# A written-out order that reaches further, two batches' k and v in other buffers, and one chunk decoded once: slot attention with a Gelu feed-forward on one core

## The chip, the cores and the metric

The kernel runs on one core of a Trainium2 chip. The core has a matrix engine (TensorE, PE in the profile; its weight loads are PEld), a vector engine (VectorE, DVE), a scalar engine with function tables (ScalarE, ACT), a general engine (GpSimd, POOL) and SyncE (SP), which here issues all data transfers (DMA). Each engine takes its instructions in the order of its own queue and waits on semaphores for the others. The metric is the device time of the whole program in microseconds (us).

## What is computed

The input has 8 batches of 8 heads, 576 positions, 64 features a head; `phi` gives each position 32 weights over memory slots.

```python
a = softmax(phi, axis=2)                       # over the positions
k_m = einsum('bhsm,bhsd->bhmd', a, k)          # 32 slots per head
v_m = einsum('bhsm,bhsd->bhmd', a, v)
attn = softmax(scale * q @ k_m^T)              # over the 32 slots
x = (attn @ v_m), heads side by side           # 4608 x 512
out = gelu(x @ w_in) @ w_out                   # 512 -> 2048 -> 512
```

The softmaxes subtract their maxima and add 1e-9 to their sums. The two weight matrices come as float64. Each is read as pairs of 32-bit words and decoded on the core into float32 parts.

## The kernel before

**Work per batch.** `x @ w_in` is never formed by itself. For each batch the kernel first folds v_m into w_in: U = v_m · w_in, one small product per head pair, in four tiles of 512 hidden columns (`U`, 8 KB a partition each, split into a high and a low part). With the attention weights p (also split into high and low) a *hidden half* h.b.f.hf is six matmuls of 288 columns: for chunk f of 128 hidden units and half hf of the positions (`hidden`, line 696). ACT applies Gelu (lines 706 to 709), the result is split into gh and gl (lines 164 and 715), and a *product* p.b.f is twelve matmuls of 512 columns into four PSUM accumulators (`project`, line 728): gh with the high and low part of w_out, gl with the high part, for four blocks of 128 positions. The last 64 positions of each batch are kept in `tails` and multiplied for two batches at once behind every second batch.

**Order of the batches.** There are 16 chunks f. Batches 0 and 1 are done in two rounds, since the weights arrive and are decoded meanwhile: chunks 0 to 7 of batch 0, chunks 0 to 7 of batch 1, then chunks 8 to 15 of batch 0 and of batch 1. After the first round the accumulators are copied out as partial sums (`o.b.j.7`, tiles `part`), and added at the end of the second (`o.b.j.15`, line 766). From batch 2 on a batch runs through all 16 chunks.

**Pieces.** The program is written as small named pieces; the table near the end of the function gives what each does. Those that matter here: `Lphi`, `Lkv`, `Lq`, `Lwi`, `Lwo` load by DMA; `amax`, `aexp`, `anorm` and `Lphin`, `dg`, `pn`, `anat` are the softmax of phi, the latter four on a transposed copy `aT` (lines 353 to 380); `slots` is the product with k and v (line 397), `km` scales it, `slotsT` and `kT` turn it round; `score`, `sT`, `max`, `sub`, `exp`, `sum`, `inv`, `mul`, `pT`, `ph`, `pl` are the attention of one half (batch 0 has its own `n_` pieces); `Up`, `Uh`, `Ul` make a piece of U. `dB`, `dC`, `dG`, `dS` decode a weight chunk (ACT lines 204 and 205; DVE lines 209, 213 and 219), each for one of the two matrices (`dB.5.1`: w_out of chunk 5) or for both at once (`dB.15`); `dDi`, `dDo` add the parts on POOL, `dE` and `dF` split w_out into high (ACT or DVE) and low (line 245). `W.k.i` is one matmul on constant ones, whose result is not used. A letter behind a colon moves a piece's work to another engine (`d` DVE, `a` ACT).

**What sets the order.** `START` is a list of pieces, run in that order; their instructions are tied to it, engine by engine, by order edges. It covers everything up to h.0.13, p.0.12 and dF.15. What it does not name is put into a plan with due times and handed to the framework's scheduler, with edges that keep a piece from running more than two steps ahead. So up to about a fifth of the time the order is fixed, and behind that it is the scheduler's.

**Buffers.** Tag `U` has `NU = 5` slots of 8 KB a partition: U tiles, the raw words of a weight chunk under decoding, and batch 0's k and v lie there. Tag `kv` has `NK = 8` slots of 2 KB: one chunk of 128 positions of k and v, or one partial sum. Batches 0 and 1 leave four partial sums each there, until their second rounds end. Batch 2's k and v (five chunks for each of two groups of heads) are planned for that time. PSUM has one pair of banks for all of `slots`, `score`, `U`, `pn` and `slotsT`, two banks for hidden halves, and four accumulators. A DMA waits in SP's queue until its buffer is free, and all behind it wait too.

Of the kernel before, what the change touches and what calls it, by code (L numbers as in the profile page):

```python
# [24 lines left out]
atc.0.0.0 atc.0.0.4 W.4.16 dG.0.1 at.0.1.4 atc.0.1.4 dS.0.1 Lkv0.0.0 slots.0.0.0 W.3.1
anorm.0 km.0.0.0 Lkv0.1.0 slots.0.1.0 dDo.0 dE.0 W.3.8 W.3.9 dF.0 km.0.1.0 Lwi.0 dB.0.0
Lq.0.0 W.4.19 Lwo.1 slotsT.0.0 kT.0.0 dC.0.0 dB.1.1 Lq.0.1 dS.0.0 dG.0.0 W.3.19 dC.1.1
dS.1.1 dG.1.1 W.3.25 n_score.0 n_max.0 n_sub.0 n_score.1 dDi.0 n_exp.0 Lphi.1.0 Lwi.1
dB.1.0 Lwo.2 dB.2.1 amax.1.0 W.3.29 n_sum.0 dDo.1 aexp.1.0 n_inv.0 n_mul.0 n_max.1
n_score.2 n_sub.1 Lkv0.0.1 slots.0.0.1 dG.1.0 dC.1.0 dC.2.1 dS.2.1 dE.1 dF.1 n_exp.1  # L30
dG.2.1 km.0.0.1 dDo.2 Lkv0.1.1 n_sum.1 n_inv.1 slots.0.1.1 km.0.1.1 slotsT.0.1 kT.0.1
Lphi.1.1 W.3.34 amax.1.1 n_mul.1 dS.1.0 Lwi.2 dB.2.0 n_max.2 Up.0.0.1 Uh.0.0:d Ul.0.0
Lwi.3 n_T.0 n_sub.2 dE.2 dDi.1 n_T.1 Lwo.3 aexp.1.1 Up.0.1.1 W.2.2 n_hi.0 dC.2.0 dS.2.0
dG.2.0 n_exp.2 Uh.0.1:d Ul.0.1 dDi.2 n_lo.0 n_sum.2 n_inv.2 Lkv.1.0.0 W.2.12 at.1.0.0
Lkv.1.0.1 Lwo.4 dB.3.1 dC.3.1 dB.3.0 dG.3.1 at.1.1.0 atc.1.1.0 dF.2 atc.1.0.0 n_hi.1
h.0.0.0 dC.3.0 n_mul.2 dG.3.0 at.1.0.4 dS.3.0 Lkv.1.0.2 atc.1.0.4 dS.3.1 Lkv.1.0.3
Lkv.1.0.4 at.1.1.4 atc.1.1.4 n_lo.1 dDi.3 n_T.2 n_hi.2 dB.4.1 dC.4.1 Lkv.1.1.0 anorm.1
slots.1.0 n_lo.2 gelu.0.0.0 dDo.3 Lkv.1.1.1 km.1.0 h.0.0.1 dS.4.1 dG.4.1 Up.0.2.1
Uh.0.2:d Lwi.4 gelu.0.0.1 dE.3 gh.0.0:a h.0.1.0 Ul.0.2 gl.0.0 gelu.0.1.0 dB.4.0
Lkv.1.1.2 dF.3 Lkv.1.1.3 Lkv.1.1.4 h.0.1.1 gelu.0.1.1 Lwi.5 dC.4.0 slots.1.1 km.1.1  # L40
h.0.2.0 dG.4.0 Lwo.5 Lq.1.0 Lwi.6 dDo.4 dE.4 slotsT.1 dS.4.0 dF.4 kT.1 dB.5.0 h.0.2.1
Up.0.3.1 Uh.0.3:d Ul.0.3 gh.0.1:a gl.0.1 Lwi.7 Lwo.7 dB.5.1 dG.5.1 dDi.4 Lwi.8 dC.5.1
gelu.0.2.0 dS.5.1 dDo.5 p.0.0 score.1.0 sT.1.0.0 sT.1.0.1 max.1.0 gelu.0.2.1 gh.0.2:a
h.0.3.0 gelu.0.3.0 sub.1.0 Lwo.6 gl.0.2 h.0.3.1 Up.0.4.1 gelu.0.3.1 p.0.1 dG.5.0 dC.5.0
dS.5.0 Uh.0.4 Ul.0.4 exp.1.0 sum.1.0 inv.1.0 mul.1.0 h.0.4.0 gh.0.3:a dB.6.0 gl.0.3
dC.6.0 dE.5 dF.5 gelu.0.4.0 dDi.5 dB.6.1 h.0.4.1 Up.0.5.1 Uh.0.5:d Ul.0.5 p.0.2 Lq.1.1
score.1.1 dG.6.0 dS.6.0 dDi.6 pT.1.0 sT.1.1.0 sT.1.1.1 max.1.1 gelu.0.4.1 dB.7.0 h.0.5.0
gelu.0.5.0 ph.1.0 gh.0.4 dG.7.0 dC.6.1 h.0.5.1 Up.0.6.1 dS.6.1 Uh.0.6 Ul.0.6 sub.1.1
p.0.3 gl.0.4 dC.7.0 dS.7.0 gelu.0.5.1 dDi.7 gh.0.5:a gl.0.5 dG.6.1 h.0.6.0 Up.1.0.4
p.0.4 h.0.6.1 gelu.0.6.0 dB.7.1 Uh.1.0 Ul.1.0 dC.7.1 Up.0.7.1 exp.1.1 Uh.0.7 p.0.5  # L50
dS.7.1 dDo.6 dE.6:d dF.6 dG.7.1 gelu.0.6.1 gh.0.6:a dDo.7 dE.7 sum.1.1 Ul.0.7 inv.1.1
h.0.7.0 gelu.0.7.0 Lwo.8 dB.8.1 mul.1.1 pl.1.0 pT.1.1 gl.0.6 Up.1.4.4 dF.7 dC.8.1
h.0.7.1 gelu.0.7.1 gh.0.7:a dS.8.1 ph.1.1:d h.1.0.0 gl.0.7 Uh.1.4:d p.0.6 Lwo.9 pl.1.1
dB.8.0 dC.8.0 dS.8.0 dG.8.1 p.0.7 Lwi.9 o.0.0.7 h.1.0.1 gelu.1.0.0 dB.9.0 dB.9.1
gelu.1.0.1 h.1.1.0 dC.9.1 dS.9.1 o.0.1.7 h.1.1.1 gh.1.0 gl.1.0 dG.8.0 Ul.1.4 dC.9.0
o.0.3.7 dDo.8 dS.9.0 dE.8:d gelu.1.1.0 gelu.1.1.1 gh.1.1 o.0.2.7:a p.1.0 h.1.2.0
gelu.1.2.0 gl.1.1 dDi.8 dG.9.0 h.1.2.1 gelu.1.2.1 dF.8 Lwi.10 dB.10.0 dC.10.0 Lwi.11
gh.1.2 dS.10.0 gl.1.2 Lwo.10 dB.10.1 p.1.1 h.1.3.0 dC.10.1 dG.9.1 dDi.9 dDo.9 h.1.3.1
gelu.1.3.1 Lwi.12 gelu.1.3.0 gh.1.3:a gl.1.3 p.1.2 h.1.4.0 h.1.4.1 gelu.1.4.0 dE.9:d
gelu.1.4.1 h.1.5.0 dS.10.1 Lwo.11 p.1.3 Lwo.12 dG.10.0 dDi.10 dG.10.1 gelu.1.5.0  # L60
gh.1.4:a gl.1.4 dF.9 dB.11.0 h.1.5.1 p.1.4 dDo.10 dE.10:d h.1.6.0 dF.10 gelu.1.5.1
gh.1.5 gl.1.5 Lwi.13 p.1.5 dC.11.0 dB.11.1 dS.11.0 dG.11.0 dB.12.1 dC.12.1 dG.12.1
dB.12.0 dC.11.1 dDi.11 dS.11.1 gelu.1.6.0 h.1.6.1 gelu.1.6.1 dG.11.1 Lwo.13 Up.0.8.4
gh.1.6:a gl.1.6 h.1.7.0 dDo.11 dE.11 h.1.7.1 dS.12.1 gelu.1.7.0 dF.11 dB.13.0 gelu.1.7.1
dDo.12 dE.12 Uh.0.8:d p.1.6 dC.13.0 Lwo.14 Ul.0.8 h.0.8.0 dG.12.0 Lwi.14 h.0.8.1
gelu.0.8.0 dC.12.0 h.0.9.0 dB.13.1 gh.1.7 gl.1.7 gelu.0.9.0 dG.13.0 Up.1.8.4 dS.12.0
gelu.0.8.1 gh.0.8:a gl.0.8 dDi.12 dC.13.1 dS.13.1 p.1.7 o.1.0.7:a dG.13.1 dS.13.0 dDi.13
o.1.1.7 Uh.1.8 Ul.1.8 h.0.9.1 Lwo.15 h.0.10.0 gelu.0.9.1 gh.0.9:a gl.0.9 o.1.2.7:a
gelu.0.10.0 dF.12 h.0.10.1 gelu.0.10.1 o.1.3.7 p.0.8 dB.14.1 gh.0.10 dC.14.1 Up.0.12.2
dDo.13 dB.14.0 dE.13:d dS.14.1 p.0.9 Lwi.15 h.0.11.0 dF.13 Uh.0.12 dG.14.1 gl.0.10  # L70
# [9 lines left out]
def slot_attention_gelu_ffn(  # L80
# [180 lines left out]

    def load_kv(b, g, c):
        rows = rows_of(b, c)
        t = sb.tile([P, 2, 4, D], F32, tag="kv", name=f"kv_{b}_{g}_{c}", bufs=NK)
# [1 line left out]
        nc.sync.dma_start(t[:rows], kv[b, g, r : r + rows])
# [698 lines left out]
```

## Time and profile before

| | |
|---|---|
| median of 3 runs | 732.03 us (731.23 to 732.37) |
| the profiled execution: its own time | 731.3 us |
| its span (first to last instruction) | 729.5 us |
| granted clock of PE, mean | 0.986 |
| PE busy | 710.9 us (97%), 4998 matmuls |
| DVE busy | 391.4 us (54%) |
| ACT busy | 333.3 us (46%) |
| POOL busy | 47.1 us (6%) |
| moved by DMA | 65.15 MB |

A line of the profile names a source line, an engine, an operation, the tile written and the tile read, sizes and a count. In a timeline the first two numbers are start and duration in us, and a bracket at the end gives how long the engine had been idle and who released it. In a table of windows each row begins with the stretch and its length; then come busy times of the engines, PE's granted clock, the share of the DMA engines and GB/s. Matmuls overlap in the records, so the durations of single matmuls add up to more than the time they take, and a busy PE is not always a PE at its pace: a product of twelve matmuls takes 2.77 us when nothing holds it.

### The profile page before, as it was taken

How to read it: one execution, taken by the hardware profiler on the slowest of the kernel's cores; microseconds unless marked ns; L12 is line 12 of the kernel's file. 1: busy time of each engine (PE TensorE's matmuls, PEld its weight loads, DVE VectorE, ACT ScalarE, POOL GpSimd, SP SyncE). 2: the span in 40 equal slices, each digit the busy share in tenths (PEclk: the TensorE clock that was granted, in tenths of full speed). 3: DMA queues.
4: the chain of work that ended last, by engine and by line, in shares of the span. 5: the costliest groups of instructions: out<-in, count | busy, mean ns of one | idle time of the engine just before them, and what ended most of it. 6: DMA issues, size and time to landing. Idle time of an engine off the chain costs nothing.

```text
span 729.5 us, 12271 instructions
## 1 busy us (share of the span) xinstructions
PE 710.9 (97%) x4998; PEld 582.9 (80%) x4998; DVE 391.4 (54%) x701; ACT 333.3 (46%) x694; POOL 47.1 (6%) x45
## 2 busy tenths in 40 slices
...
GB/s 317 294 334 30 88 202 142 73 0 203 124 106 90 178 100 59 65 175 62 33 1 81 173 63 33 1 206 62 1 1 59 48 33 1 1 58 0 1 1 72
DMA packets 28760, 65.15 MB, mean 89 GB/s; under 512 B 2848, under 2 KB 6560, under 8 KB 28704
## 3 DMA queue, kind: packets, MB, share of 16 engines
...
q14 instruction: 17, 0.14, 0.1%
...
## 4 chain that ended last, share of the span: by engine, by line
PE 91%; DMA 4%; DVE 2%; ACT 1%; issue 1%; SPq 0%; ACTq 0%; DVEq 0%
PE acc L728 48%; PE h L696 28%; PE tacc L728 6%; PE pu L457 5%; DMA kv<-kv 2%; DMA raw<-w_out 1%; PE psc L397 1%; PE psc L457 1%; PE pk L397 1%; DVE o L766 0%; PE pt L337 0%; DVE raw L213 0%; PE tn L369 0%; DVE aT L376 0%; PE tn L423 0%
## 5 line engine op out<-in xcount | busy, mean ns | idle before, releaser
L696 PE MATMUL h<-p_hi,U 128*128 128x288 f32 x1024 | 205.5, 299 | 4.0 <-ACT tails L709 4.0
L728 PE MATMUL acc<-wo_hi,gh 128*128 128x512 f32 x512 | 204.1, 399 | 0.0
L728 PE MATMUL acc<-wo_lo,gh 128*128 128x512 f32 x512 | 201.4, 393 | 0.0
L728 PE MATMUL acc<-wo_hi,gl 128*128 128x512 f32 x512 | 201.2, 394 | 0.1
L696 PEld LDWEIGHTS h<-p_hi,U 128*128 128x128 f32 x1024 | 164.6, 189 | 22.3 <-ACT tails L709 6.1
L706 ACT ACTIVATE gf<-h 128x288 f32<-128x288 f32 x128 | 52.7, 412 | 240.0 <-issue 169.5
L164 DVE CAST gh<-gf 128x512 fp32r<-128x512 f32 x115 | 48.8, 425 | 195.8 <-ACT gf L708 194.4
L728 PEld LDWEIGHTS acc<-wo_hi,gh 128*128 128x128 f32 x512 | 96.4, 188 | 36.8 <-DVE gh L164 7.5
L728 PEld LDWEIGHTS acc<-wo_hi,gl 128*128 128x128 f32 x512 | 96.0, 188 | 23.1 <-DVE gl L715 1.0
L696 PE MATMUL h<-p_lo,U 128*128 128x288 f32 x512 | 109.7, 296 | 1.3 <-DVE p_lo L552 1.3
L728 PEld LDWEIGHTS acc<-wo_lo,gh 128*128 128x128 f32 x512 | 96.4, 188 | 17.4 <-issue 0.4
L715 DVE TENSOR_TENSOR gl<-gf,gh 128x512 fp32r<-128x512 f32 x128 | 89.5, 699 | 13.9 <-ACT gh L164 5.8
L696 PEld LDWEIGHTS h<-p_lo,U 128*128 128x128 f32 x512 | 83.4, 189 | 2.2 <-DVE p_lo L552 1.5
L708 ACT ACTIVATE gf<-h 128x224 f32<-128x224 f32 x128 | 45.7, 357 | 48.3 <-PE h L696 48.2
L659 DVE TENSOR_TENSOR U<-pu,U 128x1024 fp32r<-128x1024 f32 (+2 forms) x39 | 40.1, 1029 | 15.1 <-ACT U L164 15.0
L706 ACT ACT_TABLE_LOAD x27 | 34.6, 1283 | 11.1 <-issue 6.3
L457 PE MATMUL pu<-w_in_sb,kT 64*32 64x512 f32 (+2 forms) x624 | 37.0, 531 | 0.4 <-POOL w_in_sb L239 0.4
L164 ACT CAST U<-pu 128x1024 fp32r<-128x1024 f32 (+2 forms) x31 | 29.3, 944 | 16.2 <-PE pu L457 16.2
L709 ACT ACTIVATE tails<-h 128x64 f32<-128x64 f32 x128 | 28.5, 222 | 0.0
L565 DVE STREAM_TRANSPOSE sT<-psc 128x288 f32<-128x288 f32 x28 | 11.9, 462 | 30.4 <-PE psc L397 24.5
L204 ACT ACTIVATE y<-raw 128x512 f32<-128x512 f32 (+1 forms) x33 | 22.8, 690 | 8.8 <-DMA raw<-w_out 3.2
L239 POOL TENSOR_TENSOR w_in_sb<-y,raw 128x512 int32<-128x512 int32 x16 | 22.7, 1418 | 57.2 <-DVE y L219 35.9
...
## 6 DMA issues: line engine op xcount, KB each, us to landing
kv<-kv SPq DMA_DIRECT2D x68, 256.0 KB, 5.1
...
```

The source lines that it names most:

```text
L164: return e.copy(dst, src) if e is nc.scalar else e.tensor_copy(dst, src)
L204: nc.scalar.activation(y, high.bitcast(F32), AF.Abs, scale=2.0**16)
L239: nc.gpsimd.tensor_tensor(w, y, low, op=ALU.add)
L397: nc.tensor.matmul(pk[32 * j : 32 * j + 32, w0 * D : (w0 + n) * D], st["aT", b][:rows, c, g, 32 * j : 32 * j + 32], t[:rows, w0 : w0 + n, ...
L457: nc.tensor.matmul(ps[g][M * j : M * j + M], st["kT", b][rows, t, M * j : M * j + M], moving[rows, j, :], start=True, stop=True,)
L659: nc.vector.tensor_sub(u[:, :, 1], st["pu", b, f], u[:, :, 0].bitcast(F32))
L696: i = nc.tensor.matmul(h[:, :HS], u[g][w], x[:, g, :], start=(n == 0), stop=(n == 3 * G - 1))
L706: nc.scalar.activation(gf[:, :HS], h[:, :HS], AF.Gelu)
L708: nc.scalar.activation(gf[:, HS:], h[:, : MAIN - HS], AF.Gelu)
L709: nc.scalar.activation(tails()[:, f, b % 2], h[:, MAIN - HS : HS], AF.Gelu)
L715: nc.vector.tensor_tensor(g_of("gl", b, f), g_of("gf", b, f), g_of("gh", b, f).bitcast(F32), op=ALU.subtract)
L728: nc.tensor.matmul(acc, x, w[:, f, :], start=(first and n == 0), stop=(last and n == 2))
```

## The change

Three things are changed.

1. `START` is replaced by a longer list in another order. It now reaches p.1.15, the last product of batch 1's second round. The additional pieces are those that the plan held: the last chunks of batches 0 and 1, batch 2's preparation (phi, k, v, slots, scores, p, and the first U tile) and the first loads of batch 3. In the part that both lists cover, pieces change places, 17 of the 20 `W` pieces are gone, and some 45 pieces change between ACT and DVE.
2. `load_kv` puts chunks 0 to 3 of batch 2's k and v, for each of the two groups, into one tile of tag `U`. Chunk 4 stays in a `kv` slot.
3. `dB.15`, `dC.15`, `dS.15` and `dG.15`, which decode both matrices of chunk 15 although `dB.15.0` to `dG.15.1` have done so, are no longer in the list.

The beginning of the new list (up to h.0.0.0), its part from p.0.10 on and the edit of `load_kv`:

```diff
-Lphi.0.1 W.4.2 W.4.3 W.4.5 Lphi.0.0 W.4.7 W.4.9 W.4.11 W.4.12 Lwo.0 amax.0.1 aexp.0.1
-W.4.13 amax.0.0 aexp.0.0 W.4.14 dB.0.1 dC.0.1 at.0.0.0 at.0.1.0 atc.0.1.0:d at.0.0.4
...
-gh.0.12:a dG.15.1 dS.14.0 dB.15 dG.14.0 gl.0.12 p.0.11 dC.15 dS.15 dDi.14 Up.0.14.2
-Uh.0.14:d p.0.12 dDo.14 dE.14:d dG.15 h.0.13.0 Ul.0.14 h.0.13.1 gelu.0.13.0 gelu.0.13.1
-gh.0.13 gl.0.13 dF.14 dDo.15 dE.15:d dF.15
+W.4.3 Lphi.0.0 amax.0.0 aexp.0.0 at.0.0.0 Lphi.0.1 amax.0.1 aexp.0.1 anorm.0 atc.0.0.0:d
+at.0.1.0 atc.0.1.0 at.0.0.4 Lwo.0 at.0.1.4 atc.0.1.4:d Lkv0.0.0 Lkv0.1.0 atc.0.0.4:d
+slots.0.0.0 Lwo.1 Lq.0.0 Lq.0.1 dB.0.1 dC.0.1 dG.0.1 dS.0.1 dDo.0 dE.0:d dF.0
+slots.0.1.0 km.0.0.0 km.0.1.0 Lwi.1 dB.1.1 W.4.13 dC.1.1 dS.1.1 dG.1.1 dDo.1 dE.1:d dF.1
+slotsT.0.0 kT.0.0 n_score.0 n_max.0 n_sub.0 dB.1.0 dC.1.0 dS.1.0 n_score.1 dG.1.0 Lwi.0
+n_exp.0 n_sum.0 W.3.29 dB.0.0 n_inv.0 dC.0.0 dS.0.0 Lkv0.0.1 dG.0.0 slots.0.0.1 km.0.0.1
+n_max.1 n_sub.1 n_exp.1 n_mul.0 Lkv0.1.1 slots.0.1.1 Lphi.1.0 amax.1.0 n_sum.1 Lwi.2
+km.0.1.1 Lphi.1.1 n_inv.1 n_mul.1 dDi.0 Lwo.2 slotsT.0.1 kT.0.1 aexp.1.0 Up.0.0.1
+Lkv.1.0.0 dDi.1 dB.2.0 Uh.0.0:d Ul.0.0 dC.2.0 amax.1.1 aexp.1.1 dG.2.0 dS.2.0 Lkv.1.0.1
+n_score.2 Up.0.1.1 Uh.0.1:d Lkv.1.0.2 Lwo.3 n_T.0 n_T.1 Ul.0.1 dDi.2 Lkv.1.0.3 n_max.2
+n_sub.2 dB.2.1 dG.2.1 dC.2.1 at.1.1.0 dS.2.1 n_hi.0 at.1.0.0 Lkv.1.0.4 n_lo.0 h.0.0.0
...
+gh.0.11 dC.15.1 p.0.10 dC.14.0 dS.14.0 dDi.14 aexp.2.0 Lkv.2.0.3 Lkv.2.0.2 Ul.0.12
+Lkv.2.0.0 h.0.12.0 gl.0.11 h.0.12.1 gelu.0.12.1 gelu.0.12.0 gh.0.12:a dC.15.0 aexp.2.1
+dG.15.0 p.0.11 h.0.13.0 dS.15.0 gl.0.12 dS.14.1 dDi.15 Up.0.14.2 h.0.13.1 dS.15.1 dg.2
+Lkv.2.0.1 Uh.0.14:d Ul.0.14 dDo.14 gelu.0.13.1 gelu.0.13.0 gh.0.13 gl.0.13 p.0.12
+h.0.14.0 dG.15.1 dDo.15 h.0.14.1 gelu.0.14.0 h.0.15.0 Lq.2.0 p.0.13 dE.14 gelu.0.14.1
+h.0.15.1 pn.2 Lkv.2.0.4 dF.14 gelu.0.15.0 h.1.8.0 gelu.0.15.1 gh.0.14 gl.0.14 gh.0.15:a
+dE.15 anat.2 p.0.14 h.1.8.1 gelu.1.8.1 gl.0.15 Lkv.2.1.0 dF.15 p.0.15 o.0.0.15
+gelu.1.8.0 gh.1.8 o.0.1.15 o.0.2.15 h.1.9.0 h.1.9.1 gelu.1.9.1 slots.2.0 anorm.2 km.2.0
+gelu.1.9.0 gl.1.8 h.1.10.0 gelu.1.10.0 Lkv.2.1.1 Lkv.2.1.4 gh.1.9:a gl.1.9 Lkv.2.1.2
+Lkv.3.0.0 Up.1.12.4 o.0.3.15 p.1.8 p.1.9 Uh.1.12 Lkv.2.1.3 Ul.1.12 slots.2.1 h.1.10.1
+gelu.1.10.1 km.2.1 slotsT.2 h.1.11.0 kT.2:d score.2.0 gelu.1.11.0 h.1.11.1 gelu.1.11.1
...
+inv.2.1 gelu.1.14.0 mul.2.1 gelu.1.14.1 gh.1.14 pT.2.1 gl.1.14 ph.2.1 h.1.15.0 amax.3.0
+h.1.15.1 gelu.1.15.0 pl.2.1 p.1.14 gelu.1.15.1 gh.1.15 amax.3.1 gl.1.15 tg.1.0 p.1.15
```

```diff
     def load_kv(b, g, c):
         rows = rows_of(b, c)
-        t = sb.tile([P, 2, 4, D], F32, tag="kv", name=f"kv_{b}_{g}_{c}", bufs=NK)
+        if b == 2 and c < NT:
+            t = tile_of(
+                ("kvU", g),
+                lambda: sb.tile([P, NT, 2, 4, D], F32, tag="U", name=f"kvU_2_{g}", bufs=NU),
+            )[:, c]
+        else:
+            t = sb.tile([P, 2, 4, D], F32, tag="kv", name=f"kv_{b}_{g}_{c}", bufs=NK)
```

More of the change, by code (lines that the diff above doesn't have):

```diff
@@ L22 @@
 START = """
-Lphi.0.1 W.4.2 W.4.3 W.4.5 Lphi.0.0 W.4.7 W.4.9 W.4.11 W.4.12 Lwo.0 amax.0.1 aexp.0.1
-W.4.13 amax.0.0 aexp.0.0 W.4.14 dB.0.1 dC.0.1 at.0.0.0 at.0.1.0 atc.0.1.0:d at.0.0.4
[L25 to L70, printed above, removed]
@@ L71 @@
-dB.15.0 dC.15.0 gelu.0.11.0 Ul.0.12 dG.15.0 h.0.11.1 gelu.0.11.1 dS.15.0 dDi.15 dB.15.1
-dC.15.1 dS.15.1 gh.0.11 gl.0.11 h.0.12.0 gelu.0.12.0 dC.14.0 h.0.12.1 gelu.0.12.1 p.0.10
-gh.0.12:a dG.15.1 dS.14.0 dB.15 dG.14.0 gl.0.12 p.0.11 dC.15 dS.15 dDi.14 Up.0.14.2
-Uh.0.14:d p.0.12 dDo.14 dE.14:d dG.15 h.0.13.0 Ul.0.14 h.0.13.1 gelu.0.13.0 gelu.0.13.1
-gh.0.13 gl.0.13 dF.14 dDo.15 dE.15:d dF.15
+W.4.3 Lphi.0.0 amax.0.0 aexp.0.0 at.0.0.0 Lphi.0.1 amax.0.1 aexp.0.1 anorm.0 atc.0.0.0:d
+at.0.1.0 atc.0.1.0 at.0.0.4 Lwo.0 at.0.1.4 atc.0.1.4:d Lkv0.0.0 Lkv0.1.0 atc.0.0.4:d
@@ new lines @@
+Lkv.1.0.0 dDi.1 dB.2.0 Uh.0.0:d Ul.0.0 dC.2.0 amax.1.1 aexp.1.1 dG.2.0 dS.2.0 Lkv.1.0.1
+n_score.2 Up.0.1.1 Uh.0.1:d Lkv.1.0.2 Lwo.3 n_T.0 n_T.1 Ul.0.1 dDi.2 Lkv.1.0.3 n_max.2
+n_sub.2 dB.2.1 dG.2.1 dC.2.1 at.1.1.0 dS.2.1 n_hi.0 at.1.0.0 Lkv.1.0.4 n_lo.0 h.0.0.0
+atc.1.1.0 Lkv.1.1.0 atc.1.0.0:d at.1.0.4 n_exp.2 n_sum.2 n_inv.2 n_mul.2 atc.1.0.4:d
+dB.3.1 n_hi.1 dC.3.1 dDo.2 dG.3.1 dS.3.1 dDo.3 anorm.1 at.1.1.4 n_T.2 atc.1.1.4
+gelu.0.0.0 n_hi.2 Lwi.3 slots.1.0 km.1.0 Lkv.1.1.1 n_lo.2 n_lo.1 h.0.0.1 dB.3.0 dC.3.0
@@ new lines @@
+dS.3.0 dE.2 Up.0.2.1 Lkv.1.1.2 gelu.0.0.1 Lwo.4 Uh.0.2 Lkv.1.1.3 h.0.1.0 gelu.0.1.0
+h.0.1.1 dG.3.0 dF.2 Ul.0.2 gh.0.0:a gl.0.0 dB.4.1 dC.4.1 dG.4.1 Lkv.1.1.4 slots.1.1
+h.0.2.0 dS.4.1 km.1.1 slotsT.1 kT.1:d Lwi.4 dDi.3 Lwi.5 Lq.1.0 gelu.0.1.1 gh.0.1:a
+dB.4.0 h.0.2.1 Up.0.3.1 p.0.0 gl.0.1 dE.3 dG.4.0 dDo.4 dE.4 dF.4 gelu.0.2.1 Uh.0.3
+Ul.0.3 score.1.0 dC.4.0 dS.4.0 Lwi.6 gelu.0.2.0 h.0.3.0 Lwo.7 gh.0.2:a dF.3 dB.5.0
+gelu.0.3.0 h.0.3.1 dDi.4 dB.6.0 sT.1.0.1 Lwo.5 dB.5.1 sT.1.0.0 Lwi.8 Up.0.4.1 p.0.1
@@ new lines @@
+dC.5.0 dS.5.0 dG.5.0 Uh.0.4:d Ul.0.4 h.0.4.0 gelu.0.3.1 gh.0.3:a max.1.0 dG.6.0 Lq.1.1
+dDi.5 Up.0.5.1 h.0.4.1 sub.1.0 exp.1.0 gl.0.2 dC.6.0 gl.0.3 dG.5.1 dC.5.1 dS.5.1 sum.1.0
+gelu.0.4.1 p.0.2 Uh.0.5:d Ul.0.5 inv.1.0 dDo.5 dE.5 mul.1.0 dS.6.0 score.1.1 pT.1.0
+Lwo.6 dB.6.1 Lwo.8 sT.1.1.0 p.0.3 sT.1.1.1 gelu.0.4.0 Lwi.7 gh.0.4:a dF.5 dB.7.1 gl.0.4
+dG.6.1 dDi.6 Up.0.6.1 Uh.0.6 ph.1.0:d dC.7.1 h.0.5.0 h.0.5.1 dB.7.0 Ul.0.6 dC.6.1
+max.1.1 dG.7.0 gelu.0.5.1 gelu.0.5.0 Up.1.0.4 Uh.1.0 dC.7.0 dS.7.0 sub.1.1 h.0.6.0
```

27 lines of the change are left out of this document (added).

## The prediction

> **What bounds the kernel now.** I read the page first.
>
> ```profile
> span 729.5 us, 12271 instructions
> ...
> PE 91%; DMA 4%; DVE 2%; ACT 1%; issue 1%; SPq 0%; ACTq 0%; DVEq 0%
> ```
>
> The chain that ended last is TensorE (PE) for 91% of the span, so a change is worth what it takes out of the places where PE isn't packed. A busy share can't show these, so I cut the span at the starts of hidden halves and products and asked for the windows (length, then PE, PEld, DVE, ACT, POOL busy, PE clock, DMA share, GB/s).
>
> ```profile
> 0.00:34.77 34.77, 27.98 (x316) 24.01 (x317) 24.01 (x53) 20.58 (x44) 8.70 (x13) 0.78 0.90 306
> 19.77:36.84 17.07, 15.05 (x158) 11.91 (x157) 16.64 (x39) 12.43 (x27) 3.87 (x3) 0.50 0.90 284
> 34.77:47.65 12.88, 11.11 (x156) 8.53 (x155) 11.69 (x25) 10.87 (x27) 5.47 (x4) 0.92 0.92 318
> 47.65:87.38 39.73, 39.73 (x316) 30.71 (x309) 38.31 (x71) 31.09 (x62) 9.57 (x7) 1.00 0.34 117
> 136.20:156.16 19.96, 19.96 (x119) 16.65 (x117) 16.87 (x28) 10.73 (x20) 4.96 (x4) 1.00 0.00 1
> 156.16:163.21 7.05, 4.21 (x17) 3.65 (x16) 2.01 (x6) 4.46 (x10) 0.00 (x0) 0.76 0.00 0
> 163.21:188.16 24.95, 23.61 (x208) 16.58 (x206) 10.90 (x19) 6.44 (x14) 0.31 (x1) 1.00 0.60 193
> ```
>
> Before 34.77 us, where the first hidden half (h.0.0.0) starts, nothing runs at PE's pace: DMA is 90% busy. From there to p.1.0, the first product of batch 1 at 87.38 us, DVE is busy 38.31 of 39.73 us beside a PE without gaps, so both bind. Then PE alone binds, but for 156 to 188 us, where two things go wrong. The first is on ACT:
>
> ```profile
> 154.56 1.28 ACT L380 ACT_TABLE_LOAD   x1
> 155.86 1.50 ACT L380 ACTIVATE aT<-aT 64x256 f32<-64x256 f32 x2
> 157.27 0.76 ACT L312 ACTIVATE phi<-phi,nm 128x576 f32<-128x576 f32 x1
> 157.93 0.18 ACT L312 ACTIVATION_READ_ACCUMULATOR phi<-phi,nm 128x1 f32 x1
> 158.13 1.28 ACT L708 ACT_TABLE_LOAD   x1
> 159.43 0.36 ACT L708 ACTIVATE gf<-h 128x224 f32<-128x224 f32 x1
> 159.68 0.22 ACT L709 ACTIVATE tails<-h 128x64 f32<-128x64 f32 x1
> 159.79 0.42 ACT L706 ACTIVATE gf<-h 128x288 f32<-128x288 f32 x1
> ```
>
> Between two Gelus ACT goes to Exp and back, 4.87 us (159.43 - 154.56). The other timelines show what follows (PE, DVE and SP rows):
>
> ```profile
> 159.95 0.85 PE L696 MATMUL h<-p_hi,U 128*128 128x288 f32 x2 [2.83 <-ACT tails L709]
> 163.08 0.69 DVE L766 TENSOR_TENSOR o<-acc,part 128x512 f32<-128x512 f32 x1 [0.47 <-PE acc L728]
> 163.80 8.64 SPq L266 DMA_DIRECT2D kv<-kv  x9
> 166.58 0.43 PE L397 MATMUL pk<-kv,aT 128*32 128x128 f32 x8
> 170.61 0.42 PE L397 MATMUL pk<-kv,aT 128*32 128x128 f32 x8 [0.31 <-DMA kv<-kv]
> 180.74 0.42 PE L397 MATMUL pk<-kv,aT 128*32 128x128 f32 x8 [0.98 <-DMA kv<-kv]
> ```
>
> PE stands 2.83 us and comes back at a lower clock (0.76 over that window). The second: all eight kv buffers hold the partial sums of batches 0 and 1, so batch 2's k and v start to load only when the adds of line 766 free them (add from 163.08, first issues from 163.80), and the slots of batch 2 then follow the loads piece by piece.
>
> How much both cost: what the two windows hold, at packed rates. The chain of waits gives packed pieces, the windows of lines 728 and 696 alone the counts (x45, x48):
>
> ```profile
> 43.98 1.36 PE pk L397 x40
> ...
> 46.34 0.22 PE tn L423 x2
> 188.22 1.02 PE pu L457 x16
> 193.25 0.65 PE psc L457 x16
> 193.90 0.72 PE h L696 x4
> 194.62 2.77 PE acc L728 x12
> 197.39 1.59 PE h L696 x12
> 208.83 8.16 PE tacc L728 x36
> 163.21:188.16 24.95, 12.11 (x45) 7.52 (x43) 1.00 0.60 193
> 163.21:188.16 24.95, 8.23 (x48) 6.93 (x48) 1.00 0.60 193
> ```
>
> A product is 2.77 us (0.231 a matmul), a hidden half 0.795. Window 163.21 to 188.16: 45 x 0.231 = 10.4, 48 x 0.1325 = 6.36, two slots 2.72, one U 1.02, one score 0.65, tn 0.22: 21.4 of 24.95 us, so 3.6 lost. Window 156.16 to 163.21: 12 hidden matmuls 1.59 and four of a product 0.92: 2.5 of 7.05, so 4.5 lost. Together **8.1 us**.
>
> **The change part by part.**
>
> *Batch 2's loads.* Chunks 0 to 3 of k and v go into two weight buffers (tag U, five slots). When the list reaches them, the U tile of chunks 8 to 11 of batch 0 has been read (h.0.11.1 stands ahead) and raw 14 and 15 end soon, so a slot is there each time. Chunk 4 still has a kv buffer, though, and its load stands on SP ahead of all of group 1. It waits for o.0.0.15. From the start of p.0.15: three matmuls 0.69, about 0.2 to wake DVE, the add 0.69: issue at +1.6. The first such load was issued at 163.80 and used at 166.58, 2.8 us; the median of the form is the upper bound:
>
> ```profile
> kv<-kv SPq DMA_DIRECT2D x68, 256.0 KB, 5.1
> ```
>
> So chunk 4 lies there at +4.4 to +6.7. PE wants it after p.0.15 (2.77), two halves (1.59) and 32 of 40 slot matmuls (1.09), at +5.45: a stall of 0 to 1.3 us; I take 0.6, between the two. Group 1's loads, behind it, are wanted only after another half, a U and two products (+13) and are hidden.
>
> *The Exp trips.* The list now has three: phi of group 0, phi of group 1, aT. By the rows a table switch takes 1.30 (158.13 to 159.43), phi 0.86 (157.27 to 158.13), aT 1.41 (155.86 to 157.27): trips of 3.46, 3.46 and 4.01 us in place of one of 4.87 and a shorter one. Their cover: after gelu.0.11.1 ACT has nothing due until h.0.12.1, a product and two halves later (4.36 > 3.46). The second follows gelu.0.12 and gh.0.12; h.0.14.0, which needs those buffers back, comes two products and a U later. The third must end before h.1.9.0, after pn, two halves and two products (7.7); ACT has the rest of one Gelu (0.36 + 0.22), gh and dE (two casts, taken at phi's 0.76), the trip (4.01) and a whole Gelu (0.42 + 0.58) ahead of that, 7.1. All fit, the third by 0.6 us, so I leave 0.5 us for it; were the covers missed as at 156 us, where 4.87 - 2.83 = 2.0 was covered, the three would stall 1.4 + 1.4 + 2.0 = 4.8. The Trainium skill ("ScalarE: Activation LUTs", What ACT_TABLE_LOAD costs) puts 1283 ns for the load and about 1380 ns for a drain on each switch; the load agrees with 1.28 here, the drain isn't seen (1.30 from load to next Gelu). By it each trip would be 2.7 us longer and none would fit.
>
> Late stage: -8.1 + 0.6 + 0.5 = **-7.0 us**; bounds -8.1 and -3.3 (the trips stalling 4.8).
>
> *Chunk 15 once.* Off go three double-width DVE operations, two ACT ones. They lie in 136 to 156 us, where PE is busy 19.96 of 19.96 us and DVE has 3 us free: 0 at both ends, while PE sets the pace there.
>
> *The new order before p.0.8.* Ahead of the last v load SP had the first phi of batch 1 (288 KB) and w_out 2 (512 KB); both now come behind: 0.8 MB at the 306 GB/s of the first window, 2.6 us. That is the lower bound. It is not kept in full, because DVE is full from about 20 us on and h.0.0.0 waits for n_lo.0 on DVE. Each piece at the mean of its row:
>
> ```profile
> L715 DVE TENSOR_TENSOR gl<-gf,gh 128x512 fp32r<-128x512 f32 x128 | 89.5, 699 | 13.9 <-ACT gh L164 5.8
> L164 DVE CAST gh<-gf 128x512 fp32r<-128x512 f32 x115 | 48.8, 425 | 195.8 <-ACT gf L708 194.4 <-PE acc L728 1.2
> L659 DVE TENSOR_TENSOR U<-pu,U 128x1024 fp32r<-128x1024 f32 x29 | 35.4, 1221 | 15.0 <-ACT U L164 15.0
> L213 DVE SCALAR_TENSOR_TENSOR raw<-raw 128x512 int32<-128x512 int32 x32 | 24.1, 756 | 0.4 <-ACT raw L205 0.4
> ```
>
> Between p.0.0 and p.1.0 the list loses gh three times, dE twice (a cast like gh), Uh and Ul of U.1.4, an eviction (like gl), dC.9.0 and dS.9.0 (like gh): 7 x 0.425 + 2 x 1.22 + 0.70 = 6.1 us. It gains gl.0.1, dG three times, dF twice, amax.2.1, two evictions (all six like gl), dC and dS twice and six short casts or small U pieces (all ten like gh): 6 x 0.70 + 3 x 0.756 + 10 x 0.425 = 10.7. So 4.6 us more; but most of this stood ahead of p.0.0 before, and over the whole list ahead of p.1.0 the two orders differ in DVE by a few casts against evictions and one U, about +0.4. With p.1.0 still bound by DVE and PE, I take **0** for this part. Upper bound: p.0.0 no earlier, so 4.6 less the 1.4 that DVE had idle, less the 1.6 of two halves (h.1.2) that now run ahead of p.1.0, +1.6; and one more clock window at half rate, by the second window's five steps 3.4 us each, +1.7: +3.3.
>
> *Warm-up.* 17 of 20 one-shot matmuls on `one` go. They fill PE gaps before 34.77 us, where PE has 6.8 us idle: 0, unless the clock falls with them (a rival below).
>
> *Behind p.1.15* all instructions are the same, in the scheduler's order again: 0, within 1 us either way.
>
> **Sum.** The profiled execution took 731.3 us, its span 729.5 and 1.8 around it; the median of the runs shown, 732.03, lies 0.7 above. 731.3 - 7.0 = 724.3, on the median's scale **725.0**; its own range 722.5 to 727.5.
>
> **Rivals.**
> - *Early gain kept* (722.4): the 2.6 us of the DMA carry through. For: the first stage is DMA's, 90%. Against: DVE's 38.31 of 39.73.
> - *Exp trips stall PE* (729): -8.1 + 0.6 + 4.8 = -2.7 on 732. For: this wait exists, 2.83 us. Against: each trip is shorter and stands next to finished Gelus; the drain named above would be this case, and the trace hasn't it.
> - *The loads gain nothing* (728): SP runs in order, and if chunk 4 or a weight slot holds the rest until p.0.15, the slots stall 3.6 as before: -7.0 + 3.6 - 0.6 = -4.0 on 732. For: one SP queue, and group 1 stands behind the chunk that waits. Against: five slots and two U tiles just read.
> - *DVE loses the early stage* (728.3): +3.3 on the forecast. For: DVE has 4.6 us more between p.0.0 and p.1.0. Against: its work ahead of p.1.0 is the same.
> - *Half clock* (735, the slower side): without warm-ups the sparse PE of the first 35 us leaves the clock at 0.50, and the gaps between hidden halves up to p.0.0 (11.11 busy of 12.88) and a DVE-bound start of products keep it there. Each us past 36.84 costs 0.5: until 57 us it costs 10, 725 + 10. It decides from 36.84 + 14 = 51 us on. For: 17.07 us at 0.50 though PE was 88% busy. Against: the clock came back at 36.84, 2.07 us after the first hidden half. The Trainium skill ("TensorE: Matmul & The Clock Gate", Part 1) gives one busy window of about 3.4 us for the return and one idle one for the fall; by it the loss would end within 1.7 us.
>
> **How the numbers follow.** Forecast 0.50, early gain 0.13, trips 0.12, loads 0.08, DVE 0.07, half clock 0.10. About 0.2% (1.5 us) is what a measurement of this kernel can tell from no change. The first five are all faster (0.90); each of the three at 728 to 729 has an upper part over 730.5, so I give 0.81 to faster, 0.08 to the same, 0.11 to slower. The range runs from the sum of the lower bounds (732 - 2.6 - 8.1 - 1 for what lies behind) to the trips with the early stage's +1.6 on top: 720 to 731.5.
>
> **What would show it.** Right: no PE wait of 2 us or a clock under 1.0 after 60 us; slots of group 0 at most 1.3 us late on kv; the tail products of batch 1 starting near 202 instead of 208.83; p.1.0 within 2.5 us of 87.4. Wrong: gaps of h on ACT near an Exp load; a clock of 0.50 past 45 us; p.1.0 after 91 us; kv loads of group 1 landing after p.1.9.

## The result and the profile after

The changed kernel takes 723.1 us in the median of 4 runs (722.43 to 724.85), the kernel before 731.81 us beside it (4 runs, 731.23 to 732.37). The ratio is 0.9889 (0.9873 to 0.9906): 8.7 us less, where 7.0 were forecast. Measured a second time, beside the third group of experiments, it was 723.22 against 731.36 us, ratio 0.9886 (0.9867 to 0.9906). The profiled execution took 722.78 us, its span is 721.0, so it shows 8.5 us of the 8.7.

From the page of the changed kernel, the span and the chain of work that ended last:

```profile
span 721.0 us, 12203 instructions
...
PE 92%; DVE 3%; DMA 2%; issue 1%; ACT 1%; SPq 1%; POOL 0%; DVEq 0%; ACTq 0%; POOLq 0%
```

The share of PE hardly changed (91% to 92%), as the prediction warned. The gain is in the windows (length, then busy time of PE, PEld, DVE, ACT, POOL, PE clock, DMA share, GB/s), cut in the changed kernel at its own h.0.0.0, p.0.0, p.1.0, p.0.10 and the tail products of batch 1:

```profile
0.00:32.80 32.80, 25.05 (x282) 21.14 (x283) 22.54 (x50) 15.88 (x34) 7.80 (x12) 0.72 0.96 336
32.80:46.20 13.40, 11.52 (x157) 8.46 (x155) 11.03 (x30) 11.58 (x28) 5.41 (x4) 0.93 0.64 227
46.20:88.40 42.20, 41.51 (x329) 31.98 (x321) 40.58 (x79) 33.52 (x68) 12.71 (x11) 1.00 0.42 159
133.50:199.73 66.23, 66.23 (x486) 54.32 (x479) 44.92 (x80) 33.58 (x66) 5.58 (x5) 1.00 0.33 108
```

The last row is the reading that matters: from p.0.10 to the tail products PE is busy 66.23 of 66.23 us at the full clock. Before, the stretch 156.16 to 188.16 alone had lost 8.1 us by the prediction's count.

What PE waited for behind p.0.0 (us in total, times, longest), first before, from 47 us on:

```profile
PE h L696 <- ACT tails L709: 4.0, 3, 2.8
PE pk L397 <- DMA kv<-kv: 1.3, 2, 1.0
```

and in the changed kernel, from 46.2 us on:

```profile
PE h L715 <- ACT tails L728: 1.2, 2, 0.6
PE psc L476 <- issue: 0.6, 1, 0.6
```

The wait of 2.8 us on ACT and both waits on k and v are gone. Of what is left, 0.6 lies between p.0.0 and p.1.0 and 1.2 behind the tail products.

Where on the way the 8.5 us were won shows in the PE timelines. Before, at p.0.8:

```profile
126.66 0.40 PE L728 MATMUL acc<-wo_hi,gh 128*128 128x512 f32 x1
```

In the changed kernel, at p.1.0 and at p.0.8:

```profile
88.40 0.40 PE L747 MATMUL acc<-wo_hi,gh 128*128 128x512 f32 x1
125.76 0.40 PE L747 MATMUL acc<-wo_hi,gh 128*128 128x512 f32 x1
```

and, from its chain of waits, at the tail products of batch 1:

```profile
199.89 8.16 PE tacc L747 x36
```

p.0.8 is 0.90 us earlier, with the same products and hidden halves ahead of it and 17 warm-ups less. The tail products start at 199.89 instead of 208.83, 8.94 earlier. Between the two PE has the same matmuls in both kernels. So 8.04 us come from between the two, 0.90 from ahead, and behind them 0.4 is given back.

### The profile page after: what moved, and what is told of

Its sections match the earlier page's. It is cut to its first block, busy times and chain, and to the rows that moved or that the text cites. A ratio compares the mean times of both kernels' runs of the same rounds, so it can differ in the third digit from the quotient of the medians.

```text
span 721.0 us, 12203 instructions
## 1 busy us (share of the span) xinstructions
PE 704.9 (98%) x4964; PEld 579.0 (80%) x4964; DVE 391.3 (54%) x700; ACT 332.9 (46%) x692; POOL 49.1 (7%) x45
## 4 chain that ended last, share of the span: by engine, by line
PE 92%; DVE 3%; DMA 2%; issue 1%; ACT 1%; SPq 1%; POOL 0%; DVEq 0%; ACTq 0%; POOLq 0%
PE acc L747 48%; PE h L715 28%; PE tacc L747 6%; PE pu L476 4%; PE pk L416 1%; PE psc L416 1%; PE psc L476 1%; DMA kv<-kv 1%; PE psc L493 1%; DMA raw<-w_in 1%; DVE raw L226 0%; DVE gl L734 0%; PE tn L388 0%; POOL w_in_sb L252 0%; DVE aT L395 0%
## 5 line engine op out<-in xcount | busy, mean ns | idle before, releaser
L177 DVE CAST gh<-gf 128x512 fp32r<-128x512 f32 x109 | 46.8, 430 | 189.3 <-ACT gf L727 187.7
L734 DVE TENSOR_TENSOR gl<-gf,gh 128x512 fp32r<-128x512 f32 x128 | 93.1, 727 | 11.2 <-ACT gh L177 2.9
L177 ACT CAST U<-pu 128x1024 fp32r<-128x1024 f32 (+1 forms) x31 | 29.6, 956 | 10.9 <-PE pu L476 10.7
L252 POOL TENSOR_TENSOR w_in_sb<-y,raw 128x512 int32<-128x512 int32 x16 | 24.3, 1524 | 43.7 <-DVE y L232 26.5
L217 ACT ACTIVATE y<-raw 128x512 f32<-128x512 f32 x32 | 21.6, 676 | 9.8 <-issue 4.1
```

What stands on the lines that cost most here:

```text
L177: return e.copy(dst, src) if e is nc.scalar else e.tensor_copy(dst, src)
L217: nc.scalar.activation(y, high.bitcast(F32), AF.Abs, scale=2.0**16)
L252: nc.gpsimd.tensor_tensor(w, y, low, op=ALU.add)
L734: nc.vector.tensor_tensor(g_of("gl", b, f), g_of("gf", b, f), g_of("gh", b, f).bitcast(F32), op=ALU.subtract)
```

## The experiments

All kernels here compute the whole reference. Times are medians beside the kernel before on the same chip, which took 731.49 us in the first group (the two on the loads, the late order, the first early mix), 732.31 in the second (trips, chunk 15, the first two on warm-ups) and 731.36 in the third.

### The loads alone

The old list with the edit of `load_kv`:

```diff
 START = (the old list)
...
-        t = sb.tile([P, 2, 4, D], F32, tag="kv", name=f"kv_{b}_{g}_{c}", bufs=NK)
+        if b == 2 and c < NT:
+            t = tile_of(("kvU", g), lambda: sb.tile([P, NT, 2, 4, D], F32, tag="U", ...))[:, c]
```

> The old list and only the edit of load_kv. Theory: the slots of batch 2 no longer wait (3.6 us lost between 163.2 and 188.2 us), but the Exp trip of 4.87 us still stalls a hidden half and lowers the clock (4.5 us): 731.8 - 3.6 = 728.2, if the scheduler keeps its places. Rival 1: both stalls hang on the late loads, and this alone gives 7 to 8 us, 724. Rival 2: the loads stay where the plan has them and gain nothing, 731.8.

Measured: 725.58 us (725.18 to 726.53), ratio 0.9920 (0.9900 to 0.9939), so 5.9 us less, well over the 3.6 that the prediction had put on the late slots. The PE timeline of this kernel:

```profile
157.19 1.08 PE L403 MATMUL pk<-kvU,aT 128*32 128x128 f32 x32 [0.32 <-ACT aT L386]
159.74 0.53 PE L702 MATMUL h<-p_hi,U 128*128 128x288 f32 x2 [1.46 <-ACT tails L715]
```

and two windows of it, the second from its p.0.15 on (columns as above):

```profile
156.00:163.00 7.00, 5.22 (x56) 4.29 (x55) 3.24 (x8) 4.41 (x10) 0.00 (x0) 1.00 0.01 2
160.63:185.00 24.37, 24.37 (x203) 18.58 (x202) 14.10 (x27) 9.42 (x21) 0.30 (x1) 1.00 0.45 155
```

With k and v there in time, the scheduler runs the slots while ACT is still on its Exp trip. The 2.83 us wait becomes 0.32 + 1.46 = 1.78, and the clock stays at 1.00. From p.0.15 on PE is busy 24.37 of 24.37 us. So my two losses were not apart: the late loads also left PE without work during the trip. Of the 8.1 us, 1.78 remain, which gives 6.3 for the loads; 5.9 were measured.

### The new list without the buffers

```diff
 START = (the new list)
...
-        if b == 2 and c < NT:
-            t = tile_of(("kvU", g), ...)[:, c]
-        else:
-            t = sb.tile([P, 2, 4, D], F32, tag="kv", name=f"kv_{b}_{g}_{c}", bufs=NK)
+        t = sb.tile([P, 2, 4, D], F32, tag="kv", name=f"kv_{b}_{g}_{c}", bufs=NK)
```

> The new list whole, with all of batch 2's k and v in the eight small buffers again. Theory: the eight partial sums hold the buffers until the adds behind p.0.15, the slots of batch 2 run late again by about 3.6 us, and the pinned order behind them waits in place: 723.1 + 3.6 = 726.7, up to 729 if the fixed order makes more wait. Rival: the place in the list is what matters and the buffers nothing: 723.1.

Measured: 741.05 us (738.63 to 744.1), ratio 1.0130 (1.0104 to 1.0157), 9.6 us slower than before. The direction against the changed kernel was expected, the size (up to 729) was far off. From the timelines of SP and PE in this kernel:

```profile
159.73 5.74 SPq L279 DMA_DIRECT2D kv<-kv  x4
170.01 11.62 SPq L279 DMA_DIRECT2D kv<-kv  x4
167.91 1.51 PE L410 MATMUL pk<-kv,aT 128*32 128x128 f32 x24 [2.82 <-DMA kv<-kv]
186.64 1.08 PE L410 MATMUL pk<-kv,aT 128*32 128x128 f32 x16 [4.96 <-DMA kv<-kv]
```

and the window around the first waits:

```profile
164.49:174.73 10.24, 5.63 (x62) 3.07 (x62) 1.03 (x3) 0.92 (x2) 0.00 (x0) 0.50 0.69 237
```

SP stands 5.74 and 11.62 us over its loads until buffers come free. PE, whose order is pinned, waits in place: 11.4 us in four waits (two are shown), with the clock at 0.50 for 10.24 us around the first ones. Of the 18.2 us by which its span (739.2) is longer than the changed kernel's, 11.4 are these waits and 1.5 a later start (p.0.0 at 47.72 instead of 46.20); the other 5.3 fit the half clock, these 10.24 us and 6.83 more around the last wait (PE is busy 5.63 and 5.12 us in them, and half of that is 5.4). Under the old list, where the scheduler chose, the slots had lost 3.6 by the prediction's count. The pinned order lets nothing else go ahead, so the list costs 9.6 us without the buffers, and brings some 2.8 us (8.7 - 5.9) on top of them.

### The Exp trips joined

```diff
-dDi.14 aexp.2.0 Lkv.2.0.3
+dDi.14 Lkv.2.0.3
...
-dC.15.0 aexp.2.1 dG.15.0
+dC.15.0 dG.15.0
...
-dE.15 anat.2 p.0.14
+dE.15 anat.2 aexp.2.0 aexp.2.1 p.0.14
```

> The changed kernel with one edit of its list: both aexp of batch 2 stand directly behind anat.2, so that ACT makes one long Exp trip in place of three. Theory (the prediction's sum of what covers the third trip, 7.1 of 7.7 us, with two times 0.86 us added): 8.8 against 7.7 us, PE waits about 1.1 us, 723.1 + 1.1 = 724.2; 725 if the clock falls too. Rival 1: the place of the trips is the whole of what the new late order gives beyond the loads (725.6 with the loads alone): 725.6. Rival 2: two table switches fewer outweigh it, 723.1 or less.

Measured: 724.65 us (723.07 to 724.95), ratio 0.9894 (0.9872 to 0.9916). ACT and PE of this kernel:

```profile
153.44 1.28 ACT L399 ACT_TABLE_LOAD   x1
157.77 1.28 ACT L727 ACT_TABLE_LOAD   x1
159.06 0.36 ACT L727 ACTIVATE gf<-h 128x224 f32<-128x224 f32 x1
159.59 0.53 PE L715 MATMUL h<-p_hi,U 128*128 128x288 f32 x2 [0.19 <-ACT tails L728]
```

One trip of 5.62 us, longer than the 4.87 of before, and PE waits 0.19. From p.0.15 to p.1.8 it takes 8.12 us where the changed kernel takes 7.66; so 0.46 us were lost where 1.1 were expected. The span ends 0.3 us later (721.3 against 721.0). The times alone settle little: the interval holds the changed kernel's 0.9889, and the 0.9920 of the loads alone lies 0.0004 outside it. By the trace, splitting the trip in three saves at most 0.5 us. The place of the trip saves more: behind two finished hidden halves and two products, PE has work enough for nearly the whole of it.

### Chunk 15 decoded twice again

```diff
-h.0.14.0 dG.15.1 dDo.15 h.0.14.1
+h.0.14.0 dG.15.1 dB.15 dC.15 dS.15 dG.15 dDo.15 h.0.14.1
```

> The changed kernel with the second decoding of chunk 15 put back into the list (dB.15, dC.15, dS.15, dG.15 behind dG.15.1). Theory: ACT 2.3 us and DVE 4.3 us lie beside products and PE sets the pace: 0, 723.1, at most 0.5 more. Rival: they stand ahead of dDo.15, dE.15 and the third Exp trip, whose spare was 0.6 us: 1 to 2 us more, 724.5.

Measured: 724.25 us (723.82 to 725.04), ratio 0.9894 (0.9872 to 0.9915): nothing that can be told from 0.9889. The trace does show a small place, in PE's timeline:

```profile
148.77 1.06 PE L716 MATMUL h<-p_hi,U 128*128 128x288 f32 x4
```

Such four take 0.70 elsewhere; the second half of h.0.14 is held 0.36 us in its middle. From p.0.10 to the tail products this kernel takes 66.76 us, the changed one 66.39, so that is the whole price of the second decoding in this trace, against my 0.

### The early order, from three sides

First, the old order up to p.0.10 (with its warm-ups), and all that is new behind it:

```diff
-W.4.3 Lphi.0.0 amax.0.0 aexp.0.0 at.0.0.0
...
-Up.0.12.2 Uh.0.12:d gelu.0.11.1 gh.0.11 dC.15.1
+Lphi.0.1 W.4.2 W.4.3 W.4.5 Lphi.0.0
...
+h.0.12.1 gelu.0.12.1 Lphi.2.1 amax.2.1 Lphin.2 Lphi.2.0 amax.2.0 dG.14.0
 p.0.10 dS.14.0 dDi.14 aexp.2.0 Lkv.2.0.3
```

> The old order (with its warm-up matmuls) up to p.0.10, from there the new order, batch 2's k and v in weight buffers, chunk 15 once. Theory: of the 8.7 us gained, about 1 comes from the stage before p.0.10 (p.0.10 starts 2.70 us earlier in the changed kernel, but with two hidden halves of 0.795 us less behind it) and 7.7 from the stage behind it. So this kernel is 7.7 us faster than before, 724.1. Rival: the early order carries half or more of the gain, and this kernel is at 727 or above.

Measured: 723.11 us (722.74 to 726.95), ratio 0.9892 (0.9869 to 0.9914). That can't be told from the changed kernel's 0.9889: within some 1.6 us, the half-width of the interval, the late part alone brings the gain.

Second, the reverse, the new order up to p.0.10, the old rest and the old buffers:

```diff
 gelu.0.11.0 Up.0.12.2 Uh.0.12:d gelu.0.11.1 gh.0.11 dC.15.1
-p.0.10 dC.14.0 dS.14.0 dDi.14 aexp.2.0
+dS.14.1 dC.15.0 Ul.0.12 dG.15.0 dS.15.0 dDi.15 dS.15.1 gl.0.11 h.0.12.0 gelu.0.12.0
...
```

> The new order up to p.0.10, from there the old list and the scheduler, k and v of batch 2 in their old buffers, chunk 15 decoded again. Theory: only the early part of the gain is left, about 1 us: 730.7, with the 2.8 us wait of a hidden half near 156 us and the slots late on k and v still there. Rival: the early order is worth half of the gain, 727.5.

Measured: 733.86 us (732.39 to 736.07), ratio 1.0030 (1.0015 to 1.0044). PE of this kernel shows that the seam costs most of it:

```profile
136.44 0.50 PE L695 MATMUL h<-p_hi,U 128*128 128x288 f32 x2 [1.01 <-DVE U L163]
138.29 0.79 PE L695 MATMUL h<-p_hi,U 128*128 128x288 f32 x4 [1.08 <-DVE U L658]
```

U is needed in h.0.12.0 right behind its making: 2.1 us of waits that neither order has. So a third kernel puts the product between them:

```diff
 gh.0.11 dC.15.1
+p.0.10
 dS.14.1 dC.15.0 Ul.0.12 dG.15.0 dS.15.0 dDi.15 dS.15.1 gl.0.11 h.0.12.0 gelu.0.12.0 dC.14.0 h.0.12.1 gelu.0.12.1
-p.0.10
 gh.0.12:a
```

> The new order up to and including p.0.10 and the old one behind it, with the old buffers: the first such mix put a piece of U directly ahead of h.0.12.0 and lost 2.1 us there; here the product stands between. Theory (early order worth nothing): 731.5 to 732.5 us, no PE wait over 0.5 us at h.0.12. Rival (the early order gains its DMA time, 2.6 us): 729 us. Rival (it costs DVE time): 734 us.

Measured: 732.53 us (731.23 to 735.56), ratio 1.0013 (1.0000 to 1.0027). The waits at h.0.12 are gone, but another seam has come up, and the old long Exp trip stands as before:

```profile
143.99 0.67 PE L457 MATMUL pu<-w_in_sb,kT 64*32 64x256 f32 x16 [1.72 <-POOL w_in_sb L239]
162.39 0.60 PE L696 MATMUL h<-p_hi,U 128*128 128x288 f32 x2 [2.58 <-ACT tails L709]
```

Without its seam each mix lies near the kernel before: +2.2 with 2.1 of waits, +1.2 (732.53 - 731.36) with 1.7. By this reckoning the early order is worth 0 within about 1 us. Neither 2.6 us less nor 3.3 more can be seen.

### The warm-up matmuls

None at all, and the 17 put back into the new list (one-shot matmuls ahead of both first slots, of `slotsT` and of the first score):

```diff
-W.4.3 Lphi.0.0 amax.0.0
+Lphi.0.0 amax.0.0
...
-dB.1.1 W.4.13 dC.1.1
+dB.1.1 dC.1.1
...
-n_sum.0 W.3.29 dB.0.0
+n_sum.0 dB.0.0
```

> The changed kernel without its last three warm-up matmuls. Theory: 0, 723.1; one of them takes 0.5 us in the chain of the start, so up to 0.5 less. Rival (warm-up keeps the clock): the clock falls earlier and more of the start runs at half of it, 724 or more.

```diff
-atc.0.0.4:d slots.0.0.0
+atc.0.0.4:d W.4.101 W.4.102 W.4.103 W.4.104 W.4.105 W.4.106 W.4.107 W.4.108 slots.0.0.0
...
-dF.0 slots.0.1.0
+dF.0 W.4.111 W.4.112 W.4.113 W.4.114 slots.0.1.0
...
-slotsT.0.0 kT.0.0 n_score.0
+W.4.121 W.4.122 slotsT.0.0 kT.0.0 W.3.131 W.3.132 W.3.133 n_score.0
```

> The changed kernel with 17 warm-up matmuls on ones put back into the gaps of PE ahead of the first scores (eight ahead of slots.0.0.0, four ahead of slots.0.1.0, two ahead of slotsT.0.0, three ahead of n_score.0). Theory (the prediction): 0, 723.1, since the start is bound by DMA and DVE. Rival: the first two scores, 7.06 us at half clock in the changed kernel's chain, then run at the full clock, the k and v behind them come up to 2 us earlier, 721.5, and the runs scatter less than 722.4 to 724.9.

Measured: none 723.80 us, ratio 0.9888 (0.9865 to 0.9910); 17 back 722.49 us, ratio 0.9870 (0.9845 to 0.9895). The second left a gain open, so the changed kernel, the same kernel with 17, and one with 12 more were run side by side. The 12:

```diff
-slots.0.0.1 km.0.0.1
+W.3.141 W.3.142 W.3.143 W.3.144 W.3.145 W.3.146 W.3.147 slots.0.0.1 km.0.0.1
...
-slotsT.0.1 kT.0.1
+slotsT.0.1 W.3.151 W.3.152 W.3.153 kT.0.1
...
-dB.2.0 Uh.0.0:d
+dB.2.0 W.3.161 W.3.162 Uh.0.0:d
```

> The changed kernel once more, beside the next two, on the same chip. Both theories: ratio to the kernel before 0.989, some 723 to 724 us. Its start is looked at: with the same list, p.0.0 began at 46.20 us in the first profile and, in the kernels that share the early list, between 46.03 and 47.68.

> The 17 one-shot matmuls put back into the new list, a second time, since 0.987 against 0.9889 left it open. Theory (they lie in PE's gaps and nothing waits for PE there): the same as the changed kernel, within 0.7 us. Rival (they keep the clock up, and with it the chain to the first product): 1 to 1.5 us faster in the median; p.0.0 at 45.7 us or earlier.

> The 17 one-shot matmuls and 12 more, between the second slots of batch 0 and the first pieces of U (19 to 26 us), where the clock is at half in every profile so far. If PE's clock sets the first product, p.0.0 comes up to 1 us ahead of 45.7 and the whole takes 721 to 722.5 us; if DVE and the loads set it, nothing changes against the kernel with 17.

Measured: 723.22 us (ratio 0.9886, 0.9867 to 0.9906), 722.73 us (0.9877, 0.9856 to 0.9898) and 723.52 us (0.9883, 0.9864 to 0.9902). The intervals overlap throughout. The kernel with 17 came out lowest twice, by 0.5 us in the common group; that it beats the changed kernel isn't shown. The traces say why so little can come of it. Of each of three kernels, a window (columns as above) and, from PE's timeline, the first matmul of p.0.0. The changed kernel, executed again:

```profile
9.91:33.80 23.89, 20.84 (x217) 17.36 (x217) 19.08 (x41) 11.54 (x27) 7.21 (x6) 0.50 1.03 367
```

```profile
46.18 0.50 PE L747 MATMUL acc<-wo_hi,gh 128*128 128x512 f32 x1
```

The kernel with 12 more:

```profile
5.37:25.85 20.48, 16.24 (x262) 14.29 (x262) 14.52 (x31) 9.45 (x21) 5.52 (x4) 1.00 1.02 378
```

```profile
46.21 0.50 PE L750 MATMUL acc<-wo_hi,gh 128*128 128x512 f32 x1
```

The kernel with 17, in its second measurement:

```profile
35.75:42.58 6.83, 6.36 (x68) 4.49 (x69) 4.83 (x15) 4.88 (x12) 1.71 (x2) 0.50 0.41 118
```

```profile
47.68 0.50 PE L749 MATMUL acc<-wo_hi,gh 128*128 128x512 f32 x1
```

With half clock from 9.91 to 33.80 us, or full clock from 5.37 to 25.85 (then half to 32.67), p.0.0 starts at the same time, 46.18 and 46.21. In both the DMA engines are full meanwhile (1.02 to 1.03). What moves p.0.0 shows in three steps, in the eleven traces of kernels that share the early list of the changed kernel (with or without warm-ups).

First, the loads of batch 0's first k and v land 6.7 to 8.5 us after their issue, and the first scores start between 13.57 and 15.57 us. From the DMA view and DVE's timeline of the changed kernel (its scores start at 14.23; the row is shown further below):

```profile
kv<-kv SPq DMA_DIRECT2D x2, 512.0 KB, 7.0
31.84 0.68 DVE L226 SCALAR_TENSOR_TENSOR raw<-raw 128x512 int32<-128x512 int32 x1
```

and of the third early kernel, with its scores from PE's timeline:

```profile
kv<-kv SPq DMA_DIRECT2D x2, 512.0 KB, 8.5
15.57 7.06 PE L474 MATMUL psc<-k_blocks,q 128*128 128x64 f32 x32 [0.72 <-ACT k_blocks L164]
33.20 0.68 DVE L213 SCALAR_TENSOR_TENSOR raw<-raw 128x512 int32<-128x512 int32 x1
```

Second, the DVE row is a step of the decoding that lies on the chain of waits. From the first scores to it 17.61 to 17.63 us pass in all eight executions that have these scores at half clock (7.06 us), and 16.80 and 17.17 in the two that have them at full clock (3.76 us; in one more the clock changes among them). Of the 3.3 us that the scores gain, 0.8 or less is left.

Third, from that row to p.0.0 it is 14.35 or 14.36 us in the four executions whose clock is full from 34.67 us on at the latest, 14.71 to 14.89 in the six with one more stretch of 3.41 us at half clock, ending between 38.29 and 41.70, and 15.74 in the kernel with 17, at half clock from 35.75 to 42.58.

So two things move p.0.0: when the first k and v land, and the clock, up to 1.4 us of it behind 35 us. The kernel that decodes chunk 15 twice and the third early kernel start it at 47.68 and 47.55 mostly for their loads, which took 8.3 and 8.5 us. Why the loads differ between executions wasn't found.

## Why the prediction held, point by point

**The late stage** was the right place and the right size: 8.1 us were forecast to be lost there, and 8.04 came back. The split into 4.5 for the Exp trip and 3.6 for the slots was wrong. The loads alone brought 5.9, because on-time slots fill the trip's wait, and then the clock doesn't fall either.

**Chunk 4's stall** (0.6 taken, 0 to 1.3) didn't come. From the timelines of SP and PE in the changed kernel:

```profile
158.20 0.33 SPq L285 DMA_DIRECT2D kv<-kv  x1
161.91 0.40 PE L416 MATMUL pk<-kv,aT 128*32 128x128 f32 x8
166.16 0.46 SPq L285 DMA_DIRECT2D kvU<-kv  x1
169.91 1.08 PE L416 MATMUL pk<-kvU,aT 128*32 128x128 f32 x32
```

and the DMA view's row for the first of these loads (KB, us to landing):

```profile
kv<-kv SPq DMA_DIRECT2D x1, 256.0 KB, 2.8
```

The load is issued 1.61 us after the start of p.0.15 (156.59), where +1.6 was worked out, and wanted at +5.32 (worked out: +5.45). It landed 2.8 us after its issue, the lower of the two times that the prediction reckoned with (2.8 and 5.1), so it was there 0.9 us early. The cover is thin for group 1 as well, which I had called hidden: in the kernel with 12 more warm-ups its last chunk, issued at the same 166.17, took 5.0 us instead of 3.7, and PE waited 0.48 us for it.

**The Exp trips** (0.5 taken) cost nothing. ACT in the changed kernel:

```profile
134.07 1.28 ACT L331 ACT_TABLE_LOAD   x1
138.15 0.36 ACT L727 ACTIVATE gf<-h 128x224 f32<-128x224 f32 x1 [0.62 <-PE h L715]
139.59 1.28 ACT L331 ACT_TABLE_LOAD   x1
143.29 0.36 ACT L727 ACTIVATE gf<-h 128x224 f32<-128x224 f32 x1 [0.23 <-PE h L715]
153.52 1.28 ACT L399 ACT_TABLE_LOAD   x1
156.34 1.28 ACT L727 ACT_TABLE_LOAD   x1
157.63 0.36 ACT L727 ACTIVATE gf<-h 128x224 f32<-128x224 f32 x1
```

After the first two trips ACT stands 0.62 and 0.23 us waiting for PE, so both fit with that to spare. The third takes 4.11 us (157.63 - 153.52; 4.01 forecast), and PE has no wait behind it. The next Gelu starts 1.29 us after the start of the load (157.63 - 156.34). The drain of some 1380 ns on each switch that the Trainium skill gives ("ScalarE: Activation LUTs", What ACT_TABLE_LOAD costs) is not seen here either.

**Chunk 15** at 0 was 0.36 off by the trace, too little for the times.

**The early order** at 0 stands within 1 us. Of the count behind it, one part came out and one didn't. Ahead of p.1.0 DVE is busy for 74.15 us in all against 74.01 before, +0.1 where +0.4 was counted. Between p.0.0 and p.1.0 it grew by 2.3 us (40.58 busy against 38.31), half of the 4.6 that the prediction added up piece by piece. p.1.0 starts 1.0 us later than before, at 88.40, inside the 2.5 allowed, with two more hidden halves (1.59) ahead of it. In the profiled executions h.0.0.0 starts 1.97 us earlier (32.80 against 34.77), near the 2.6 of the DMA, and 0.90 of it is left at p.0.8. On the way PE stands idle for 0.69 us between p.0.0 and p.1.0, where before it had no gap.

**Behind p.1.15**, 0 within 1: 0.4 was given back between the tail products and the end.

**The sum**: -7.0 became -8.5 in the profiled executions. The difference is the two reserves that weren't needed (0.6 and 0.5) and the 0.9 at p.0.8, less the 0.4 behind. The 0.9 I can't assign: the start of p.0.0 moves by 1.5 us between executions that share this early list, as the rows above show, so the profile alone can't credit it to the order.

**The rivals.** Early gain kept would have given 722.4, and 723.1 is nearer to that than to 725.0, but the mechanism isn't there: the old early order with the new late part measures 0.9892 against 0.9889. Trips that stall, loads that gain nothing and a DVE that loses the early stage are each refuted by a row above. The half clock past 40 us exists, but it ended at 34.67 us in the profiled execution of the changed kernel; behind that its clock is 1.00 in every window above that starts later.

**The range.** Its upper end, 731.5, isn't the sum that it names: the trips at 729.3 and the early stage's 1.6 give 730.9.
